# Thirteen input loads of a linear-attention kernel cut by partitions into 28 transfers

## The chip, the core and the metric

The kernel runs on one core of one Trainium2 chip. The core has five engines with queues of their own: TensorE (PE: matrix products, into PSUM), VectorE (DVE), ScalarE (ACT), GpSimd (POOL) and SyncE (SP), which here only issues transfers. Sixteen DMA engines move data between the chip's memory (HBM) and SBUF, the on-chip memory of 128 partitions. The metric is the device time of one execution in microseconds (us); less is better.

## What is computed

Two layers, one after the other: a decaying linear attention over 768 positions for 4 batches and 8 heads of 64, then a token mixer and a projection on its result.

```python
# attention: q, k, v are (4, 8, 768, 64)
for t in range(S):
    state = gamma[None, :, None, None] * state + np.einsum('bhd,bhe->bhde', k[:, :, t], v[:, :, t])
    y[:, :, t] = scale * np.einsum('bhd,bhde->bhe', q[:, :, t], state)
# x = y as (4, 768, 512); mixer:
W_tok = scale * np.einsum('bsd,btd->bst', x @ w_q, x @ w_k)
mixed = np.einsum('bst,btd->bsd', W_tok, x)
return np.maximum(mixed, 0.0) @ w_out
```

## The kernel before

The 768 positions of each batch are taken in three pairs of chunks of 128 positions, which makes twelve pairs, numbered 0 to 11; three pairs in a row belong to one batch. For each pair p the kernel needs three inputs, here called kp, qp and vp (k6 is the k input of pair 6). Each is one load of 512 KB into a staging buffer of 128 partitions: partition g holds positions 2g and 2g + 1 of the pair for all eight heads, so a partition gets eight pieces of 512 bytes. A partition of a load is called a row below.

A pair then goes through these steps. `ck`, `cq` and `cv` (L301, L329, L313) cast the loads to bf16, v with its decay factor; `ck` and `cv` come in two halves, and half c reads partitions 64c to 64c + 63 of the load (`rows(c)`). `trk` and `trq` transpose on PE and `ekT` evicts. `sc` and `eat` make the masked scores, `st` and `es` the running state, `ia` and `in` the output, `ex` takes it out of PSUM. `xt`, `exT`, `wqk`, `ew`, `zm`, `ez`, `mx` and `r` are the mixer, and `pj` and `eo` the projection with `w_out`. `stored` (L619) writes a pair's result, 512 KB, to HBM.

Nothing is scheduled automatically. `ORDER` (L16) is a list of all steps written out by hand; the letter behind a step names its engine (A for ACT, V for DVE, P for POOL), and each engine runs its own steps in the order of the list. SP's queue is written out in `LOADS` (L56): first all loads, with w (the mixer's two small weights) and o (`w_out`, in four transfers) between them, and at the end the stores s0 to s11. `more_loads` (L181) takes tokens off this list as long as the next one may go: a load of q, k or v needs a staging buffer, of which there are eighteen (`STAGES`), and a store needs its result evicted. The first k load is issued in halves, one from ACT and one from SP. On SP a transfer also waits until the transfer eight places before it has landed, since eight semaphores serve all of them in turn.

The helper that casts records its line as L135 (ACT) or L136 (POOL, DVE); `cv` is L318; loads are issued at L154, w at L162 and L163, o at L166, stores at L629.

Of the kernel before, what the change touches and what calls it, by code (L numbers as in the profile page):

```python
# [53 lines left out]


LOADS = """  # L56
q0 v0 k1 q1 v1 k2 q2 v2 w k3 q3 v3 k4 q4 v4 k5 q5 v5 o k6 q6 v6 k7 q7 v7 k8 q8 v8 k9 q9 v9 k10
q10 v10 k11 q11 v11 s0 s1 s2 s3 s5 s4 s6 s7 s8 s9 s10 s11/0 s11/1
""".split()

# [5 lines left out]
def kernel(  # L66
# [15 lines left out]
    nc = tc.nc  # L82
# [4 lines left out]
    C = 128  # L87
# [4 lines left out]
    HP = H // 2  # L92
# [51 lines left out]
    wk_stage = wstage_pool.tile([128, NDM, DH], FP32, name="wk_stage")  # L144
    wout_stage = wstage_pool.tile([128, NDM, DM], FP32, name="wout_stage")

    def load(name, p, half=None, eng=None):
        src = {"k": k, "q": q, "v": v}[name]
        b, cp = divmod(p, NP)
        st = pairs[p]  # L150
        if name + "_st" not in st:
            st[name + "_st"] = stage_pool.tile([128, 2, HP, 2, D], FP32, name=name + "_st", tag="st")
        xs = slice(0, 2) if half is None else slice(half, half + 1)
        dma = (eng or nc.sync).dma_start(  # L154
            out=st[name + "_st"][:, xs].rearrange("g x hp j d -> g (x hp) (j d)"),
            in_=src[b, xs.start * HP : xs.stop * HP, cp * 2 * C : (cp + 1) * 2 * C, :].rearrange(
                "h (g j) d -> g h (j d)", j=2
            ),
        )
    def load_token(token):  # L160
        if token == "w":
            nc.sync.dma_start(out=wq_stage, in_=moe_w_q.rearrange("(a p) h -> p a h", p=128))  # L162
            nc.sync.dma_start(out=wk_stage, in_=moe_w_k.rearrange("(a p) h -> p a h", p=128))  # L163
        elif token == "o":
            for a in range(NDM):
                nc.sync.dma_start(  # L166
                    out=wout_stage[:, a], in_=moe_w_out[128 * a : 128 * a + 128, :], max_dma_last_dim=512
                )
        else:
            load(token[0], int(token[1:]))  # L170

    load("k", 0, 0, nc.scalar)
    load("k", 0, 1, nc.sync)

    queue = list(LOADS)
    staged = ["k0"]
# [4 lines left out]
    def more_loads():  # L181
        while queue:
            token = queue[0]
            if token[0] == "s":
                if not stored(token[1:]):
                    return
                queue.pop(0)
                continue
            if token not in "wo":
                n = len(staged)  # L190
                if n >= STAGES and staged[n - STAGES] not in cast:
                    return
                staged.append(token)
            load_token(queue.pop(0))

    parts = {}
# [1 line left out]
    def release(token, n):  # L198
        parts[token] = parts.get(token, 0) + 1
        if parts[token] == n:  # L200
            cast.add(token)
            more_loads()

    more_loads()


# [7 lines left out]
    for h in range(H):  # L214
        x, hp = divmod(h, HP)
# [393 lines left out]
    def eo(e, b, p, j):  # L609
        st = pairs[p]  # L610
        if "o" not in st:
            st["o"] = ost_pool.tile([128, 2, DM], FP32, name="o_st")
        copy(e, st["o"][:, j], st["o_ps", j])
        evicted.add((p, j))
        more_loads()
# [3 lines left out]
    def stored(name):  # L619
        p, _, j = name.partition("/")  # L620
        p, js = int(p), [int(j)] if j else [0, 1]
        if not all((p, i) in evicted for i in js):
            return False
        b, cp = divmod(p, NP)
        dst = out[b, cp * 2 * C : (cp + 1) * 2 * C, :].rearrange("(g j) m -> g j m", j=2)
        src = pairs[p]["o"]
        if j:
            dst, src = dst[:, int(j)], src[:, int(j)]
        nc.sync.dma_start(out=dst, in_=src, max_dma_last_dim=512)  # L629
        return True  # L630
# [7 lines left out]
    for token in ORDER:  # L638
        token, _, b = token.partition("@")
        token, _, e = token.partition(":")  # L640
# [38 lines left out]
```

## Time and profile before

| | us |
|---|---|
| median of 3 runs | 98.48 (98.37 to 99.06) |
| the profiled execution | 98.37 |
| its span, first to last instruction | 96.6 |
| PE, DVE, ACT, POOL busy | 84.3, 75.1, 71.6, 59.5 |
| HBM read, written | 20.19 MB, 6.29 MB |
| a load, median from issue to landing | 6.3 (q), 6.5 (v), 6.4 (k) |

The profile is one execution on the chip. Its page gives, among other things, the busy tenths of each engine in 40 slices of 2.4 us, the busy share of the DMA engines and the rate that they moved (GB/s), the DMA queues, and the chain of work that ended last, followed back from the end. q1 is SP's queue, q10 ACT's, q8 and q14 carry instructions. In a timeline, a line gives the start, the duration, the engine, the line, the operation, the tiles, how many, and in brackets the idle time before it with what ended it. [...]

### The profile page before, as it was taken

To read this page: it belongs to the slowest core of one execution; us is meant where nothing else is said; L and a number is where in the kernel's file an instruction comes from. 1 tells how busy PE (TensorE), PEld (TensorE's weight loads), DVE (VectorE), ACT (ScalarE), POOL (GpSimd) and SP (SyncE) were. 2 spreads that over 40 slices of the span, in tenths; PEclk is the share of its full clock that TensorE was granted. 3 is DMA by queue.
4 is the path that set the end of the run, shared out by engine and by line. 5 is a ranking of instruction groups with operands and counts; after the bars stand their busy time and mean duration, and the time that the engine had idled before them with its cause. 6 is when DMAs were issued, how large, how long until landed. Compare 5 with 4: busy or idle time off the path is not lost.

```text
span 96.6 us, 3839 instructions
## 1 busy us (share of the span) xinstructions
PE 84.3 (87%) x1657; PEld 54.0 (56%) x1657; DVE 75.1 (78%) x108; ACT 71.6 (74%) x113; POOL 59.5 (62%) x74
## 2 busy tenths in 40 slices
PE   4999879897896789599999899999789999999920
PEld 1344355576765558256856546867776686534400
DVE  3035879999997999995798989989879997318640
ACT  4273999589797795597979999999999867454300
POOL 6610379494797997949999999999999500000000
PEclk9999999999999999999999999999999999999999
DMA  1999999989999999999999999999999980072995
GB/s 23 263 347 347 345 347 337 283 262 338 294 303 324 320 317 293 290 283 288 329 308 284 271 351 331 292 266 339 348 339 346 317 249 2 0 224 78 324 317 153
DMA packets 53137, 26.73 MB, mean 277 GB/s; under 512 B 1920, under 2 KB 53120, under 8 KB 53120
## 3 DMA queue, kind: packets, MB, share of 16 engines
q1 hardware_dynamic: 52592, 26.22, 92.3%
q10 hardware_dynamic: 528, 0.26, 0.9%
q8 instruction: 13, 0.21, 0.8%
q14 instruction: 4, 0.03, 0.1%
HBM read 20.19 MB, written 6.29 MB: 274 GB/s over the span
## 4 chain that ended last, share of the span: by engine, by line
SPq 22%; PE 22%; DMA 13%; POOL 12%; ACT 11%; DVE 10%; issue 6%; POOLq 0%; ACTq 0%; DVEq 0%
SPq L154 20%; DMA v_st<-in_v_dram 13%; PE banks L600 11%; POOL vs L318 8%; ACT ks L135 4%; POOL ks L136 4%; DVE at_sb L412 4%; DVE o_st L136 3%; ACT relu L593 2%; SPq L162 2%; PE banks L400 2%; PE banks L578 2%; PE banks L525 1%; ACT w_x L135 1%; PE banks L506 1%
## 5 line engine op out<-in xcount | busy, mean ns | idle before, releaser
L318 POOL TENSOR_TENSOR vs<-v_st,fv 64x512 bf16<-64x512 f32 x44 | 46.0, 1045 | 8.0 <-DMA v_st<-in_v_dram 3.6
L412 DVE TENSOR_TENSOR at_sb<-banks,cmask 128x1024 bf16<-128x1024 f32 x24 | 28.6, 1217 | 1.8 <-PE banks L400 1.3
L135 ACT CAST ks<-k_st 64x512 bf16<-64x512 f32 x38 | 23.4, 617 | 4.4 <-DMA k_st<-in_k_dram 3.8
L600 PE MATMUL banks<-wout_sb,relu 128*128 128x512 bf16 x96 | 23.3, 380 | 0.4 <-POOL wout_sb L136 0.4
L488 DVE TENSOR_TENSOR x_nat<-banks,fy 128x1024 bf16<-128x1024 f32 x12 | 14.6, 1220 | 1.6 <-PE banks L440 1.4
L600 PEld LDWEIGHTS <-relu 128*128 128x128 bf16 x96 | 8.2, 98 | 9.9 <-issue 1.4
L294 PE MATMUL banks<-warm 128*128 128x512 bf16 x41 | 12.6, 440 | 1.3 <-DVE warm L209 1.3
L593 ACT ACTIVATE relu<-banks 128x1024 bf16<-128x1024 f32 x9 | 9.3, 1028 | 2.2 <-PE banks L578 2.1
L135 ACT COPY o_st<-banks 128x512 f32<-128x512 f32 x15 | 8.7, 590 | 2.8 <-PE banks L600 2.8
L400 PE MATMUL banks<-qT,kT 64*128 64x128 bf16 x192 | 8.5, 216 | 1.3 <-ACT relu L593 0.8
L474 PE MATMUL banks<-vs,at_sb 128*128 128x64 bf16 x192 | 8.3, 194 | 0.4 <-DVE at_sb L412 0.4
L136 DVE COPY o_st<-banks 128x512 f32<-128x512 f32 x9 | 6.1, 686 | 2.9 <-PE banks L600 2.9
L135 ACT CAST qs<-q_st 128x1024 bf16<-128x1024 f32 (+1 forms) x8 | 7.9, 994 | 0.4 <-DMA q_st<-in_q_dram 0.3
L135 ACT COPY xT<-banks 128x1024 bf16<-128x1024 bf16 x7 | 7.2, 1022 | 1.4 <-PE banks L506 1.2
L474 PEld LDWEIGHTS <-at_sb 128*128 128x128 bf16 x192 | 6.8, 98 | 1.8 <-DVE at_sb L412 0.5
L136 DVE COPY kT<-banks 128x1024 bf16<-128x1024 bf16 x9 | 6.2, 687 | 2.1 <-PE banks L358 1.0
L136 POOL CAST qs<-q_st 128x1024 bf16<-128x1024 f32 (+1 forms) x4 | 3.7, 932 | 6.5 <-DMA q_st<-in_q_dram 6.4
L525 PE MATMUL banks<-xT,wqk_w 128*128 128x256 bf16 x48 | 7.2, 273 | 0.5 <-ACT xT L135 0.4
L400 PEld LDWEIGHTS <-kT 64*128 64x128 bf16 x192 | 6.4, 94 | 2.3 <-issue 1.8
L135 ACT CAST s_sb<-banks 128x256 bf16<-128x256 f32 x13 | 4.9, 378 | 3.2 <-PE banks L454 3.2
L294 PEld LDWEIGHTS <-warm 128*128 128x128 bf16 x41 | 3.9, 110 | 6.0 <-issue 2.7
L454 PE MATMUL banks<-vs,ks 128*64 128x64 bf16 x160 | 6.3, 200 | 0.5 <-ACT s_sb L135 0.5
(56 smaller groups left out, 112.8 us busy)
## 6 DMA issues: line engine op xcount, KB each, us to landing
q_st<-in_q_dram SPq DMA_DIRECT2D x12, 512.0 KB, 6.3
v_st<-in_v_dram SPq DMA_DIRECT2D x12, 512.0 KB, 6.5
k_st<-in_k_dram SPq DMA_DIRECT2D x11, 512.0 KB, 6.4
out_dram<-o_st SPq DMA_DIRECT2D x11, 512.0 KB, 6.1
wout_stage<-in_moe_w_out_dram SPq DMA_DIRECT2D x4, 256.0 KB, 5.6
out_dram<-o_st SPq DMA_DIRECT2D x2, 256.0 KB, 2.7
k_st<-in_k_dram ACTq DMA_DIRECT2D x1, 256.0 KB, 4.3
k_st<-in_k_dram SPq DMA_DIRECT2D x1, 256.0 KB, 4.0
```

What stands on the lines that cost most here:

```text
L135: return nc.scalar.copy(out=out, in_=in_)
L136: return ENGINES[e].tensor_copy(out=out, in_=in_)
L154: dma = (eng or nc.sync).dma_start(out=st[name + "_st"][:, xs].rearrange("g x hp j d -> g (x hp) (j d)"), in_=src[b, xs.start * HP : xs.st ...
L294: nc.tensor.matmul(out=bank32(b), lhsT=warm[:, 0:128], rhs=warm, start=True, stop=True)
L318: ENGINES[e].tensor_tensor(out=st["vs"][rows(j), c].rearrange("p hp x d -> p x hp d"), in0=st["v_st"][rows(c), :, :, j], in1=fv[rows(c), p ...
L400: nc.tensor.matmul(out=ps[:, x, hi, c, :], lhsT=st["kT"][rows(x), hp, c, :], rhs=st["qT"][rows(x), hp, c, :], start=(hi == 0 and c == 0), ...
L412: ENGINES[e].tensor_tensor(out=st["at", half].rearrange("p x hi c t -> p (x hi c) t"), in0=st["at_ps", half].rearrange("p (n t) -> p n t", ...
L474: nc.tensor.matmul(out=y[:, x, c, hp, :], lhsT=st["at", half][:, x, hi, c, :], rhs=st["vs"][:, c, hp, x, :], start=first(p, x), stop=False ...
L488: nc.vector.tensor_tensor(out=st["x"].rearrange("p x c i n -> p (x c i n)").rearrange("p (m d) -> p m d", d=D), in0=st["y_ps"].rearrange(" ...
L525: nc.tensor.matmul(out=ps[:, 128:384], lhsT=wqk_sb[:, a, 0:128], rhs=st["xT"][:, a].rearrange("p c t -> p (c t)"), start=(a == 0), stop=(a ...
L593: nc.scalar.activation(out=dst, in_=st["mx_ps"], func=ACT.Relu)
L600: nc.tensor.matmul(out=bank32(b), lhsT=st["relu"][:, a, j, :], rhs=wout_sb[:, a, :], start=(a == 0), stop=(a == NDM - 1),)
```

## The change

Each load may now be cut by partitions into several transfers. In `LOADS` a token may carry the sizes: `v3:120.8` is a transfer of partitions 0 to 119 and one of the last 8. Thirteen of the loads, v3 to q5 and v6 to v8, get sizes from six patterns: 120+8, 112+8+8, 104+24, 108+20, 110+18 and 100+28. The pieces of a load follow each other in SP's queue. The places of the loads and stores in the list, `ORDER`, the buffers and the arithmetic are the same.

```diff
 LOADS = """
-q0 v0 k1 q1 v1 k2 q2 v2 w k3 q3 v3 k4 q4 v4 k5 q5 v5 o k6 q6 v6 k7 q7 v7 k8 q8 v8 k9 q9 v9 k10
+q0 v0 k1 q1 v1 k2 q2 v2 w k3 q3 v3:120.8 k4:112.8.8 q4:104.24 v4:108.20 k5:110.18 q5:100.28 v5 o k6 q6 v6:120.8 k7:112.8.8 q7:104.24 v7:108.20 k8:110.18 q8:100.28 v8:120.8 k9 q9 v9 k10
 q10 v10 k11 q11 v11 s0 s1 s2 s3 s5 s4 s6 s7 s8 s9 s10 s11/0 s11/1
 """.split()
...
-    def load(name, p, half=None, eng=None):
+    def load(name, p, half=None, eng=None, cuts=(128,)):
...
-        dma = (eng or nc.sync).dma_start(
-            out=st[name + "_st"][:, xs].rearrange("g x hp j d -> g (x hp) (j d)"),
-            in_=src[b, xs.start * HP : xs.stop * HP, cp * 2 * C : (cp + 1) * 2 * C, :].rearrange(
-                "h (g j) d -> g h (j d)", j=2
-            ),
-        )
+        g = 0
+        for n in cuts:
+            (eng or nc.sync).dma_start(
+                out=st[name + "_st"][g : g + n, xs].rearrange("g x hp j d -> g (x hp) (j d)"),
+                in_=src[
+                    b,
+                    xs.start * HP : xs.stop * HP,
+                    cp * 2 * C + 2 * g : cp * 2 * C + 2 * (g + n),
+                    :,
+                ].rearrange("h (g j) d -> g h (j d)", j=2),
+            )
+            g += n
...
-            load(token[0], int(token[1:]))
+            token, _, cuts = token.partition(":")
+            load(token[0], int(token[1:]), cuts=[int(n) for n in (cuts or "128").split(".")])
...
-                staged.append(token)
+                staged.append(token.partition(":")[0])
```

## The prediction

> **What bounds the kernel now.** I read the page first (busy slices, queues, chain of waits), then busy time by stretches, the DMA row around single holes, SP's issues, and the stretches of POOL and ACT where a cast stands next to a landing.
>
> ```profile
> DMA  1999999989999999999999999999999980072995
> GB/s 23 263 347 347 345 347 337 283 262 338 294 303 324 320 317 293 290 283 288 329 308 284 271 351 331 292 266 339 348 339 346 317 249 2 0 224 78 324 317 153
> ...
> q8 instruction: 13, 0.21, 0.8%
> ...
> SPq 22%; PE 22%; DMA 13%; POOL 12%; ACT 11%; DVE 10%; issue 6%; POOLq 0%; ACTq 0%; DVEq 0%
> ```
>
> The sixteen DMA engines have work nearly all the time up to slice 32, and a third of the chain that ended last is SP's queue and a landing. The GB/s row shows that the stream is not at its best all that time: 345 to 347 early on, then again and again under 300. q8 are 13 fetches of 16 KB of instructions; 0.8% of 16 engines over 96.6 us is 12.4 us, so about 0.95 us each, on an engine that also carries loads.
>
> ```profile
> core 0: us, PE busy (x) PEld busy (x) DVE busy (x) ACT busy (x) POOL busy (x), PEclk, DMA share, GB/s
> 6.00:14.00 8.00, 6.95 (x99) 3.52 (x98) 4.70 (x7) 5.92 (x10) 2.70 (x3) 1.00 1.15 346
> 21.00:32.00 11.00, 9.33 (x243) 7.06 (x236) 10.29 (x13) 9.00 (x16) 8.32 (x9) 1.00 1.07 316
> ...
> 39.00:51.00 12.00, 11.11 (x229) 7.23 (x230) 10.29 (x13) 9.68 (x16) 10.17 (x12) 1.00 1.03 300
> 51.00:64.00 13.00, 12.60 (x304) 8.43 (x297) 12.13 (x15) 12.77 (x20) 12.20 (x13) 1.00 1.01 297
> 64.00:74.00 10.00, 8.97 (x204) 6.57 (x202) 8.81 (x12) 9.87 (x16) 9.41 (x10) 1.00 1.14 341
> ```
>
> Up to 51 us loads arrive at 300 to 316 GB/s with every compute engine almost full; from 51 to 74 us ACT is idle for only 0.23 + 0.13 = 0.36 us, so what makes ACT late at 51 us stays late; after that the chain of waits is PE without a break from 72.5 to 92.3 us. The clock is 1.00 throughout.
>
> The next answer is the DMA row from 18 to 22 us, 0.1 us a slice:
>
> ```profile
> DMA  9999999997658352114786899999999999999999
> GB/s 320 356 351 346 325 356 351 346 300 220 185 164 164 97 102 82 46 41 113 215 210 184 256 348 338 307 333 353 353 338 343 353 348 343 481 328 333 328 312 328
> ```
>
> Fetch number one ran at 16 to 18 us. The hole comes about 2 us later, when the other engines run dry: the shortfall against 346 from 18.8 to 20.2 us adds up to 0.8 us of stream. [...]
>
> ```profile
> 15.14 0.69 SPq L154 DMA_DIRECT2D k_st<-in_k_dram  x1
> 15.87 2.43 SPq L154 DMA_DIRECT2D q_st<-in_q_dram  x1
> 18.35 0.83 SPq L154 DMA_DIRECT2D v_st<-in_v_dram  x1
> ```
>
> [...] From 20.7 to 50.8 us the queue moved 9.29 MB, 309 GB/s in 30.1 us; at 346 it would be 26.9 us. So 3.2 us are lost there, with five fetches.
>
> ```profile
> 40.01 2.16 POOL L318 TENSOR_TENSOR vs<-v_st,fv 64x512 bf16<-64x512 f32 x2
> 43.47 2.15 POOL L318 TENSOR_TENSOR vs<-v_st,fv 64x512 bf16<-64x512 f32 x2 [1.30 <-DMA v_st<-in_v_dram]
> ```
>
> ```profile
> 50.88 1.25 ACT L135 CAST ks<-k_st 64x512 bf16<-64x512 f32 x2 [0.15 <-DMA k_st<-in_k_dram]
> ```
>
> POOL waited 1.30 us for v6 (issued at 36.73, 6.60 us to landing: 43.33) and has no further wait for a load up to 76 us; ACT waited 0.15 us for k8 (issued at 43.41, 7.4 us: 50.80). These two landings have no slack. Others have: q8 lands at 52.30 and POOL casts it at 52.75.
>
> **The change part by part.**
>
> *Same work elsewhere.* PE, DVE, ACT and POOL hold the same instructions in the same order; no step moves and the stores keep their place. Some casts wait for two or three transfers instead of one; the queue waits in the chain are 0.02 and 0.04 us, so this is nothing against a cast of 0.6 to 1.05 us.
>
> *Fifteen more issues on SP.* Thirteen loads become 28 transfers. An issue that nothing holds took 0.37 us (the late stores), so 15 x 0.37 = 5.6 us of SP's time. [...] Cost 0. [...]
>
> *A shorter window.* Eight semaphores serve the transfers in turn, so each issue waits until the one eight places before has landed. Before, eight places are eight loads, 8 x 1.49 = 11.9 us, against 6.3 us to landing: never binding. After, the tightest spot is the rest of k5, which waits for the first piece of k4 with under three loads between, 4.3 us; a load lands 4.9 us after its issue has ended (v4: 23.02 + 1.48 to 29.43). So SP is held for about 0.6 us at such a spot. [...]
>
> *Uneven pieces.* A load is 128 rows of eight 512-byte packets. At 346 GB/s it takes 1.49 us (SP's issues start 1.49 us apart from 5.3 to 9.7 us), 8 rows on each engine, 0.186 us a row. An engine has no speed in reserve: in the answer for 19.60 to 19.74 us, where one or two engines are at work (37 GB/s), packets still come about 24 ns apart, as with sixteen (512 bytes at 346/16 GB/s). So whoever gets more rows is later, and idle neighbours do not help. How a piece is shared out the trace does not show. Bound below: shared perfectly, 0 extra rows. Bound above: the large pieces rounded up to whole rows on sixteen engines, and the rests on only eight of them. Up to the first piece of k8 (that is all its first cast needs, rows 0 to 63) this is 79 + 25 = 104 rows on the busiest engine instead of 11 x 8 = 88: 16 x 0.186 = 3.0 us. I take the value between, all sixteen engines and whole rows: each of the six patterns costs its busiest engine 9 rows instead of 8 (8+1, 7+1+1, and 7+2 four times). Up to v6 that is seven split loads, +7 rows, +1.3 us; up to the first piece of k8 it is ten times +1 and then 7 for 8, +9 rows, +1.7 us; up to q8 +12 rows, 2.2 us, less 0.45 us of slack. I take it because unsplit loads run at the pace of all sixteen.
>
> *The holes.* Their cost before is 3.2 us up to k8. If the engine that fetches code is relieved, they shrink, at most by these 3.2 us; if it carries as much as any other, they stay. I keep them, since a piece of 100 to 120 rows on sixteen engines gives each engine about the same.
>
> [...]
>
> **Sum.** ACT is 1.7 us later at k8 and can swallow at most its 0.36 us of idle time by 74 us; POOL is 1.3 us later at v6 and 1.75 us at q8. The end is PE's, fed by both: +1.5 us. The profiled execution took 98.37 us (span 96.6 and 1.8 around it), 0.1 under the median of 98.48: 98.37 + 1.5 = 99.9 us.
>
> **The rivals.**
>
> *Faster: the holes close.* If the relieved engines include the one that fetches code, and pieces are shared well, up to 3.2 us of stream come back. For: a hole of 0.8 us behind a fetch is in the row above. Against: DVE is idle for only 0.71 us in 21 to 32 and 1.71 us in 39 to 51, and POOL can gain only what it waits, 1.30 us at v6 and 0.64 us for wout before. So at most about -1.7 us, 96.7 us. It decides from the point where the relief exceeds the extra rows by 1 us at v6 and k8.
>
> *No difference.* The pieces are shared evenly (0 rows, holes kept), or relief and extra rows cancel: 98.4 us. For it: most of the split loads land before their cast's turn comes, and the holes cost more (3.2 us) than nine rows do (1.7 us). Against it: the two would have to cancel at v6 and at k8 alike.
>
> *Much slower: few engines do the rests.* 3.0 us at k8 plus 0.6 us of held SP, less 0.36: +3.2 us, 101.6 us; more if several small pieces land late.
>
> **How the numbers follow.** Forecast 99.9 (99.4 to 101.0): 0.42. Much slower, 101.0 to 103.5: 0.16. No difference, 97.5 to 99.4: 0.24. Faster, 95.9 to 97.4: 0.18. Under 1% a measurement of this kernel cannot tell from no change, so faster 0.18, same 0.24, slower 0.58. The range from 96.8 to 102.4 leaves out about half of the faster case and half of the much slower one.
>
> **What would show it.** Right: between 21 and 32 us and between 39 and 51 us the stream is under 300 GB/s while DMA has slices under 9; POOL's wait for v6 grows from 1.30 to about 2.5 us, ACT's for k8 from 0.15 to 1 us or more; SP's issues of rests stay near 0.4 us. Wrong: v6 lands before 43.3 us, or the holes behind the fetches are gone, or ACT has idle time after 51 us that swallows a late k8.

## The result and the profile after

The changed kernel takes 106.52 us (median of 4 runs, 105.46 to 107.08), the kernel before took 98.43 us beside it (98.07 to 99.06): 1.078 times the time, 95% interval 1.066 to 1.090. Slower, as forecast, but by 8 us and not by 1.5; the time lies above the range. The profiled execution took 106.06 us, with a span of 104.3 us. A kernel's executions scatter, and those with a lower granted clock of TensorE are mostly the longer ones (the unchanged kernel once took 103.68 us at a mean clock of 0.956), so a ratio below counts only executions within 1.5% of the kernel's quickest, and `first` and `all104`, with one such execution each, have a median alone.

First the page of the changed kernel: the DMA row, the rate and the chain by engine, 2.6 us a slice.

```profile
DMA  1999999999987999999988999999999994053995
GB/s 25 306 347 347 347 351 315 255 245 230 170 221 209 254 304 335 331 250 220 233 203 203 203 242 293 300 339 345 341 349 339 339 316 135 0 156 100 274 318 164
...
SPq 34%; PE 24%; DMA 18%; POOL 10%; ACT 4%; issue 4%; DVE 1%; POOLq 0%; ACTq 0%; DVEq 0%
```

The rate falls to 170 to 255 GB/s where the two groups of cut loads pass (slices 8 to 14 and 18 to 24) and is at 347 to 351 before the first group and at 339 to 349 after the second. The DMA row says little of it: nearly all its digits are 9. SP's queue now has a third of the chain.

The same stretches as shown of before, with the same columns:

```profile
core 0: us, PE busy (x) PEld busy (x) DVE busy (x) ACT busy (x) POOL busy (x), PEclk, DMA share, GB/s
6.00:14.00 8.00, 6.95 (x122) 3.75 (x120) 5.19 (x6) 5.91 (x11) 3.03 (x4) 1.00 1.15 347
21.00:32.00 11.00, 7.53 (x183) 5.63 (x182) 8.82 (x11) 8.20 (x14) 5.64 (x6) 1.00 0.99 216
39.00:51.00 12.00, 9.47 (x218) 6.21 (x211) 9.20 (x11) 7.60 (x12) 7.33 (x7) 1.00 1.10 279
51.00:64.00 13.00, 9.63 (x192) 6.24 (x192) 8.85 (x12) 9.07 (x15) 9.84 (x12) 1.00 0.95 225
64.00:74.00 10.00, 9.46 (x226) 6.29 (x225) 9.00 (x13) 9.85 (x16) 9.39 (x10) 1.00 1.08 322
```

The last two columns are to be read together. The share is the time that all packets took, divided by the window, over 16 engines (it can be above 1: packets of one engine overlap, they start about 24 ns apart and take 27); so 16 x 512 bytes x share / rate is the time that one packet takes. From 6 to 14 us it is 8192 x 1.15 / 347 = 27.1 ns, as before (1.15 at 346). From 21 to 32 us before it was 8192 x 1.07 / 316 = 27.7 ns; now it is 8192 x 0.99 / 216 = 37.5 ns, and from 51 to 64 us 34.6 ns. The loss has two parts: the share is 0.99 instead of 1.15 (engines stand idle, 0.86), and a packet takes 37.5 ns instead of 27.1 (0.72); 0.86 x 0.72 = 0.62 = 216 / 347. This time per packet is the number that the rest of the study goes by.

What waits for it, in the stretches of POOL and then ACT:

```profile
43.78 2.16 POOL L327 TENSOR_TENSOR vs<-v_st,fv 64x512 bf16<-64x512 f32 x2
49.47 2.15 POOL L327 TENSOR_TENSOR vs<-v_st,fv 64x512 bf16<-64x512 f32 x2 [3.54 <-DMA v_st<-in_v_dram]
...
61.25 1.04 POOL L136 CAST qs<-q_st 128x1024 bf16<-128x1024 f32 x1 [2.56 <-DMA q_st<-in_q_dram]
```

```profile
52.76 1.04 ACT L135 CAST qs<-q_st 128x1024 bf16<-128x1024 f32 x1 [0.83 <-DMA q_st<-in_q_dram]
...
55.60 0.37 ACT L135 CAST s_sb<-banks 128x256 bf16<-128x256 f32 x1 [1.80 <-PE banks L463]
...
57.40 1.25 ACT L135 CAST ks<-k_st 64x512 bf16<-64x512 f32 x2 [0.66 <-DMA k_st<-in_k_dram]
```

v6 lands at 49.35 us instead of 43.33, the first piece of k8 at 57.32 instead of 50.80, q8 at 61.10 instead of 52.30. The chain of work that ended last runs through q8's landing (start and duration in us):

```profile
53.87 7.23 DMA q_st<-in_q_dram
61.17 0.08 issue
61.25 1.05 POOL qs L136
```

Before, the same cast started at 52.75 us:

```profile
52.75 1.04 POOL L136 CAST qs<-q_st 128x1024 bf16<-128x1024 f32 x1
```

So POOL is 8.5 us later there. It waits for nothing from there to its last cast, in either kernel, and the span ends 7.7 us later (104.3 instead of 96.6): all but 0.8 us of the delay goes to the end.

SP's issues in the second group; a line is a load's two pieces, the second figure the time that they held SP's queue (SPq):

```profile
47.60 3.17 SPq L156 DMA_DIRECT2D v_st<-in_v_dram  x2
50.87 2.48 SPq L156 DMA_DIRECT2D k_st<-in_k_dram  x2
53.45 2.60 SPq L156 DMA_DIRECT2D q_st<-in_q_dram  x2
56.14 2.46 SPq L156 DMA_DIRECT2D v_st<-in_v_dram  x2
```

A load holds the queue for 2.5 to 3.2 us instead of the 1.45 us of a whole one. That can be the fifteen further issues, or SP waiting for slower engines; the experiments had to say which.

One more view of the trace: the records of landings on the eight semaphores. A whole transfer leaves sixteen (before, each semaphore has 112 for seven transfers). In the change, a transfer with fewer than sixteen leaves one record more, 0.1 to 0.2 us after its issue ends: 1029 records in all are 1003 landings and one more for each of 26 transfers. The landings are 15 for 120 rows, 16 for 112 and 128, 13 for 104, 12 for 108, 11 for 110, 10 for 100, and 8, 12, 10, 9 and 14 for the rests of 8, 24, 20, 18 and 28. The packets of under 512 bytes on the page go with them: 2027 instead of 1920, 107 more, and by these counts thirteen loads have 315 landings instead of 208. Below, a landing is taken for one DMA engine that has done its part, and the rows of a transfer for evenly shared among its engines (each of these counts divides its row count); that is a reading of the counts. Which of the sixteen engines take part the records do not say.

### The profile page after: what moved, and what is told of

Same layout as the page of the kernel before. It is cut to its first block, busy times and chain, and to the rows that moved or that the text cites. A ratio compares the mean times of both kernels' runs of the same rounds, so it can differ in the third digit from the quotient of the medians.

```text
span 104.3 us, 3860 instructions
## 1 busy us (share of the span) xinstructions
PE 84.3 (81%) x1657; PEld 54.0 (52%) x1657; DVE 75.5 (72%) x108; ACT 71.7 (69%) x113; POOL 59.5 (57%) x74
## 2 busy tenths in 40 slices
DMA packets 53244, 26.73 MB, mean 256 GB/s; under 512 B 2027, under 2 KB 53227, under 8 KB 53227
## 4 chain that ended last, share of the span: by engine, by line
SPq 34%; PE 24%; DMA 18%; POOL 10%; ACT 4%; issue 4%; DVE 1%; POOLq 0%; ACTq 0%; DVEq 0%
SPq L156 28%; DMA q_st<-in_q_dram 14%; PE banks L609 11%; POOL vs L327 7%; DMA wout_stage<-in_moe_w_out_dram 4%; SPq L174 3%; PE banks L483 2%; ACT qs L135 2%; POOL wout_sb L136 2%; PE banks L534 2%; PE banks L587 2%; SPq L170 2%; PE banks L565 2%; PE banks L515 1%; PE banks L463 1%
## 5 line engine op out<-in xcount | busy, mean ns | idle before, releaser
L421 DVE TENSOR_TENSOR at_sb<-banks,cmask 128x1024 bf16<-128x1024 f32 x24 | 28.5, 1216 | 2.5 <-PE banks L409 2.1
L303 PE MATMUL banks<-warm 128*128 128x512 bf16 x41 | 12.0, 422 | 1.3 <-DVE warm L218 1.3
L463 PEld LDWEIGHTS <-ks 128*64 128x64 bf16 x160 | 4.8, 110 | 8.2 <-issue 7.5
L379 PE MATMUL banks<-identity,qs 64*128 64x64 bf16 x192 | 4.9, 191 | 3.0 <-POOL qs L136 1.2
```

The costliest lines, as they stand in the source:

```text
L303: nc.tensor.matmul(out=bank32(b), lhsT=warm[:, 0:128], rhs=warm, start=True, stop=True)
L421: ENGINES[e].tensor_tensor(out=st["at", half].rearrange("p x hi c t -> p (x hi c) t"), in0=st["at_ps", half].rearrange("p (n t) -> p n t", ...
L463: nc.tensor.matmul(out=state_ps[rows(x), hp, :], lhsT=st["ks"][:, c, hp, x, :], rhs=st["vs"][:, c, hp, x, :], start=(cp == 0 and c == 0 an ...
```

## The experiments

The theories after the result: *rows* (the engines that take part, and the rows on the busiest one, set the time), *issues* (fifteen more issues and the eight semaphores hold SP), *any other shape is slow*, and *sharing* (engines that are at work together slow each other down, and by how much depends on how many rows each gets; an assumption of the author's).

### Each shape by itself: shapes and shapes2

```python
for n in SHAPES:                      # shapes: 128 120 112 110 108 104 100 96 64
    for i in range(6):
        nc.sync.dma_start(out=bufs[i][0:n], in_=rows_of(src, (turn // 3) % 12, n))
    ...                               # the group is awaited, then the next shape
```
```diff
-SHAPES = (128, 120, 112, 110, 108, 104, 100, 96, 64)
+SHAPES = (128, 104, 117, 120, 105, 126, 110, 99, 64)
...
+    pool.tile([128, 224], FP32, name="pad")
```

> Loads alone, the attention and the mixer left out (the output is whatever the loads brought): nine groups of six transfers of the same shape, of 128, 120, 112, 110, 108, 104, 100, 96 and 64 rows, each group begun when the one before has landed; read by stretches. Rows theory (an engine's pace per packet is always 23 to 24 ns, and a transfer uses as many engines as its landings count: 16, 15, 16, 11, 12, 13, 10, 16, 16): rows on the busiest engine 8, 8, 7, 10, 9, 8, 10, 6, 4, so six transfers stream for 8.9, 8.9, 7.8, 11.2, 10.1, 8.9, 11.2, 6.7, 4.5 us, and the rate while streaming is 346 GB/s times the engines in use over 16 (324 for 120 rows, 216 for 100 rows). Packet theory (packets of a transfer that is not 128 rows take about a third longer, as 37 ns against 28 ns in the profile of the changed kernel): the groups other than 128 rows take a third more than that, 110 GB/s less at 112 and 96 rows than at 128.

Measured in `shapes`, as the mean duration of the group's packets, in ns: 128 rows 32.6, 120 45.7, 112 34.7, 110 32.6, 108 27.5, 104 45.7, 100 31.9, 96 39.4 (64 rows ran into the stores and cannot be separated). Neither the number of engines nor the size of a transfer orders these. The 108 rows stand out: they alone are at full pace, and they alone give an engine nine rows (108 rows, twelve landings). So `shapes2` asked for the same numbers of engines with nine rows each:

> Loads alone again (attention and mixer left out), six transfers of each shape: 128, 104, 117, 120, 105, 126, 110, 99 and 64 rows. [...] Rows theory (pace the same for all): 104 and 117 rows both at 280 GB/s, 120 and 105 both at 324. Any-other-shape theory (every transfer that is not 128 rows has slow packets): 117 and 126 as slow as 104 and 120.

The middles of its first eight groups, 128, 104, 117, 120, 105, 126, 110 and 99 rows:

```profile
core 0: us, DVE busy (x) POOL busy (x), PEclk, DMA share, GB/s
4.00:11.00 7.00, 0.00 (x0) 0.00 (x0) 1.00 1.15 347
15.00:26.00 11.00, 0.00 (x0) 0.00 (x0) 1.00 1.01 203
30.00:39.50 9.50, 0.00 (x0) 0.00 (x0) 1.00 0.93 282
43.00:55.00 12.00, 0.00 (x0) 0.00 (x0) 1.00 1.15 230
59.00:66.50 7.50, 0.00 (x0) 0.00 (x0) 1.00 1.13 290
71.00:80.00 9.00, 0.00 (x0) 0.00 (x0) 1.00 1.00 303
83.00:95.00 12.00, 0.00 (x0) 0.00 (x0) 1.00 0.82 210
100.00:109.00 9.00, 0.00 (x0) 0.00 (x0) 1.00 0.78 235
```

The second and third rows decide. A block here is the rows of a transfer that fall to one engine. On the same thirteen engines blocks of eight rows take 8192 x 1.01 / 203 = 40.8 ns a packet, blocks of nine 8192 x 0.93 / 282 = 27.0 ns: with eight rows an engine has lost about a third of its pace (27.0 / 40.8 = 0.66). Six transfers of 117 rows were through in 11.2 us, six of 104 rows in 13.2 us, so the larger transfer is the quicker one. 120 rows (blocks of eight) take 41.0 ns, 126 (blocks of nine) 27.0, and 105 (blocks of seven, if fifteen engines share them as for 120) 31.9; on eleven engines 110 rows (blocks of ten) take 32.0 and 99 (blocks of nine) 27.2. The engines of the three fast shapes can also be estimated from the table: sixteen have a share of 1.15 at that pace, so 0.93, 1.00 and 0.78 are 12.9, 13.9 and 10.9 engines. "Rows" alone and "any other shape is slow" fall. That 128 rows took 32.6 ns in one run and 27.1 in the other is not explained: the buffers lie elsewhere without the pad, and the two ran on different chips.

### On which side: source

If the eight rows of an engine follow each other, the blocks of the thirteen engines also lie 8 x 512 = 4096 bytes apart in HBM. This kernel keeps the partitions and moves the rows in HBM apart.

```diff
-SHAPES = (128, 104, 117, 120, 105, 126, 110, 99, 64)
+SHAPES = ((128, 2), (104, 2), (104, 3), (104, 5), (117, 2), (117, 3), (128, 3), (128, 5), (128, 2))
...
-        return src[b, :, cp * 256 : cp * 256 + 2 * n, :].rearrange("h (g j) d -> g h (j d)", j=2)
+        return src[b, :, 0 : n * step, :].rearrange("h (g t) d -> g h (t d)", t=step)[:, :, 0:128]
```

> Loads only, without the computation; the stores write what lies in the buffers, so the output is not the reference's. Nine groups of six transfers: 128, 104, 104, 104, 117, 117, 128, 128, 128 rows, whose rows lie 512, 512, 768, 1280, 512, 768, 768, 1280, 512 bytes apart in DRAM (the packets stay 512 bytes, and each row goes to the same partition as before). With blocks of eight rows, 512 bytes apart, thirteen engines read at distances of 4096 bytes from each other, with blocks of nine 4608 bytes: so the slow pace of 104 rows could come from the source side as well as from the partitions written. Theory 'partitions': 104 rows take 38 to 46 ns a packet, 165 to 205 GB/s, at all three distances, and 117 rows 27 to 28 ns, 280 GB/s, at both. Theory 'source': 104 rows become as fast as 117 rows (27 to 28 ns, 280 GB/s) at 768 and 1280 bytes, or 117 rows become slow at 768.

Its groups two to six: 104 rows at 512, 768 and 1280 bytes, 117 rows at 512 and 768.

```profile
core 0: us, DVE busy (x) POOL busy (x), PEclk, DMA share, GB/s
...
15.00:25.50 10.50, 0.00 (x0) 0.00 (x0) 1.00 1.00 208
30.00:40.50 10.50, 0.00 (x0) 0.00 (x0) 1.00 1.01 203
46.00:56.00 10.00, 0.00 (x0) 0.00 (x0) 1.00 1.00 202
61.00:69.50 8.50, 0.00 (x0) 0.00 (x0) 1.00 0.93 282
74.00:82.50 8.50, 0.00 (x0) 0.00 (x0) 1.00 0.93 281
```

39 to 41 ns for blocks of eight at every distance, 27 ns for blocks of nine at both. The distance in HBM does not matter at these three values, which leaves the side of the partitions; that follows by exclusion, no run moved the partitions alone.

### The same engines, other cuts: even112, half64, byhead

All three keep 28 transfers. `even112` and `half64` put eight rows on each of sixteen engines; `byhead` cuts by heads, so that every transfer has 128 partitions. Each of the three has 2160 packets of under 512 bytes, 240 more than before, which is sixteen landings for each of the fifteen further transfers.

```diff
 even112
-... v3:120.8 k4:112.8.8 q4:104.24 v4:108.20 k5:110.18 q5:100.28 ...
+... v3:112.16 k4:96.16.16 q4:112.16 v4:112.16 k5:112.16 q5:112.16 ...
 half64
+... v3:64.64 k4:64.32.32 q4:64.64 v4:64.64 k5:64.64 q5:64.64 ...
 byhead
+... v3:7.1 k4:6.1.1 q4:7.1 v4:7.1 k5:7.1 q5:7.1 ...
-                out=st[name + "_st"][g : g + n, xs].rearrange("g x hp j d -> g (x hp) (j d)"),
+                out=st[name + "_st"][:, xs].rearrange("g x hp j d -> g (x hp) (j d)")[:, g : g + n],
```

> The same thirteen loads cut into the same number of transfers (28), but 112+16, and 96+16+16 for k4 and k7: every piece is a multiple of 16 rows and loads all sixteen engines alike, 8 rows a load. Rows theory: back to the time before, 98 to 99 us. Issue theory (more transfers, SP held by the eight semaphores): still 104 to 107 us. Packet theory: packets of pieces other than 128 rows a third longer, thirteen loads of 1.49 us by a third, up to +6.5 us, 102 to 105 us.

> The thirteen loads cut 64+64 (64+32+32 for k4 and k7): the same number of transfers (28) and the same 8 rows on each of sixteen engines as without a cut. Rows theory: 98 to 99 us. Issue theory: as in the run with 112+16, 101 to 102 us. [...]

> The thirteen loads cut by heads instead of partitions: 128 rows x 7 heads and 128 rows x 1 head (6+1+1 for k4 and k7), 28 transfers as in the change, sixteen engines, 8 rows each. Issue theory (more issues and the eight semaphores cost time by themselves): 100 us or more. Rows and sharing theories: 98 to 99 us, as before.

Measured: `even112` 101.56 us (ratio 1.029, 1.020 to 1.039), `half64` 101.79 us (1.031, 1.024 to 1.038), `byhead` 99.13 us (1.004, 0.9995 to 1.008). The stretch from 21 to 32 us, first of `byhead`, then of `half64`, with the columns of the changed kernel's table:

```profile
21.00:32.00 11.00, 9.26 (x244) 7.11 (x240) 10.61 (x12) 9.71 (x17) 7.12 (x8) 1.00 0.99 289
```

```profile
21.00:32.00 11.00, 7.80 (x191) 5.85 (x189) 8.99 (x11) 8.38 (x14) 5.78 (x6) 0.99 1.19 245
```

`byhead` has as many issues and semaphores as the change, and its packets take 28.1 ns: "issues" is refuted, up to the 0.8% that the interval leaves. `half64` has no engine with more rows than before and none idle, its share is 1.19, and still the rate is 245 GB/s, because a packet takes 39.8 ns. So nearly all its loss is pace. That its time is the 101 to 102 us of "issues" is chance, since `byhead` has as many. `even112` fits none of its forecasts well: slower than "rows" had it (98 to 99 us) and a little quicker than slow packets for every other shape (102 to 105 us).

### One pattern for all: all120, all104, all117

```diff
 all120
+... v3:120.8 k4:120.8 q4:120.8 v4:120.8 k5:120.8 q5:120.8 ...
 all104
+... v3:104.24 k4:104.24 q4:104.24 v4:104.24 k5:104.24 q5:104.24 ...
 all117
+... v3:117.11 k4:117.11 q4:117.11 v4:117.11 k5:117.11 q5:117.11 ...
```

> [...] Rows theory: +1 row a load, 13 x 0.186 = 2.4 us at most, 99.5 to 101 us. Packet theory: +2.4 us and up to a third on 1.49 us thirteen times, 103 to 107 us.

> All thirteen loads are cut 104 + 24, and nothing else differs from the change. By the landing counts of the changed kernel 104 rows go to 13 engines in blocks of eight rows and 24 rows to 12 engines in blocks of two: ten rows on the busiest engines instead of eight. [...] Theory 'rows' (only the count of rows on the busiest engine matters): 2 rows x 0.186 = 0.37 us a load, 3.7 us at k8: 101 to 103 us, the same as for 117 + 11.

> All thirteen loads are cut 117 + 11: 13 engines with blocks of nine rows, and 11 engines with one row, so ten rows on the busiest engines, on the same number of engines as for 104 + 24. Theory 'sharing': no collision in the large piece, 1.7 us + 0.2 us instead of 1.5 us a load, 4 us at k8: 101 to 103.5 us, clearly below 104 + 24. Theory 'rows': the same number, and equal to 104 + 24. Theory 'any shape but 128 is slow': about 106 us, as for 104 + 24.

Measured: `all120` 104.12 us (1.056, 1.044 to 1.068), `all104` 105.9 us (103.26 to 106.72), `all117` 103.35 us (1.048, 1.039 to 1.057). `all120` lies where slow packets had it, `all117` where "sharing" had it, and `all104` above the 101 to 103 us of "rows". The stretch from 21 to 32 us of `all104`, then of `all117`:

```profile
21.00:32.00 11.00, 7.48 (x183) 5.78 (x182) 8.84 (x11) 7.80 (x13) 5.57 (x6) 0.98 0.97 199
```

```profile
21.00:32.00 11.00, 8.69 (x219) 6.67 (x218) 9.52 (x13) 8.60 (x14) 5.87 (x7) 1.00 0.83 241
```

Both put ten rows on the busiest engines (13 and 12 landings a load in `all104`, 13 and 11 in `all117`: 2037 and 2024 packets of under 512 bytes). 39.9 ns a packet with blocks of eight, 28.2 with blocks of nine, and v8 lands at 64.24 against 58.29 us. Their times overlap in part, the streams do not. That `all117` is 4.8% slower although its packets are at full pace is the other part of the loss: its share is 0.83, since three engines have nothing to do in a large piece and the busiest have two rows more.

### One group alone: first and second

```diff
 first
+... v3:120.8 k4:112.8.8 q4:104.24 v4:108.20 k5:110.18 q5:100.28 v5 o k6 q6 v6 k7 q7 v7 k8 q8 v8 ...
 second
+... v3 k4 q4 v4 k5 q5 v5 o k6 q6 v6:120.8 k7:112.8.8 q7:104.24 v7:108.20 k8:110.18 q8:100.28 v8:120.8 ...
```

> Only the first six loads cut (v3 to q5), with the patterns of the change. If the two groups of loads add up, about half of the 8 us: 101.5 to 103 us. If the first group is absorbed by the slack of v5 and o behind it and only the second one counts: 99 to 100 us. [...]

> Only the second group of loads (v6 to v8) is cut, with the patterns of the change; v3 to q5 are whole. If each group costs by itself (the delay that the first group leaves is not swallowed before the second), this takes about half of the change's 8 us, 101 to 103.5 us, and the two parts add up to the change. If the first group's delay is swallowed by idle time between the groups and only the second counts, this takes the whole, 105 to 107 us. If the second group's delay is hidden behind work that the first group has already made late, it takes under 100 us.

Measured: `first` 103.86 us (101.89 to 105.68), `second` 101.83 us (100.66 to 104.3; ratio 1.025, 1.016 to 1.034). Each group costs by itself, so neither is hidden behind the other. In the profiled runs the last of the packets up to v8 starts 3.9 us later than before in `first`, 5.6 us in `second` and 8.5 us in the change: in the stream the two parts add up to a little more than the whole. Whether the times add up as well is open: the medians are 5.4 and 3.4 us above the kernel before, against 8.1 us for the change, but each scatters by 3.6 us and more.

### An attempt to relieve the late engine: relief126

The one faster rival rested on the engine that also fetches code. In whole loads one landing often comes late (k8 before: fifteen by 49.79 us, the last at 50.80). 126 rows leave fourteen landings, with nine rows for each engine, at full pace (27.0 ns in `shapes2`). Eight loads were cut 126 + 2 in the hope that the engine that fetches would be one of the two without a part in the large piece. No trace stood behind that hope. One row more in eight loads is 8 x 0.186 = 1.5 us, against the 3.2 us of the holes.

```diff
-q0 v0 k1 q1 v1 k2 q2 v2 w k3 q3 v3:120.8 k4:112.8.8 q4:104.24 v4:108.20 k5:110.18 q5:100.28 v5 o k6 q6 v6:120.8 ...
+q0 v0 k1 q1 v1 k2 q2 v2 w k3:126.2 q3 v3 k4:126.2 q4 v4 k5:126.2 q5 v5:126.2 o k6 q6:126.2 v6 k7 q7 v7 k8 q8:126.2 v8 k9 q9:126.2 v9 k10
+q10:126.2 ...
```

> [...] If every shape but 128 is slow: 102 us or more.

Measured: 100.88 us (1.023, 1.017 to 1.029). Slower, but the late engine was not left out. The first fetch ran from 16.38 to 17.31 us, and of the fourteen landings of k3's large piece thirteen had come by 19.70 us and the last at 20.78; before, fifteen of k3's had come by 19.69 us and the last at 20.71. So the engine that fetches seems to be one of the fourteen, and late landings show as well in pieces on thirteen engines (v3 in `all117`: twelve by 23.99 us, the last at 25.16). The run shows what eight cuts of 126 + 2 cost; what a relief of that engine would bring stays untested.

### What a cut load costs with its rests: mixed

```diff
-SHAPES = (128, 104, 117, 120, 105, 126, 110, 99, 64)
+SHAPES = """
...
+126.2 126.2 126.2 126.2 126.2 126.2
+126.2 128 126.2 128 126.2 128
+104.24 104.24 104.24 104.24 104.24 104.24
...
+120.8 112.8.8 104.24 108.20 110.18 100.28
+128 128 128 128 128 128
+""".strip().splitlines()
...
+            for n in [int(c) for c in cuts.split(".")]:
+                nc.sync.dma_start(out=bufs[i][g : g + n], in_=rows_of(src, (turn // 3) % 12, g, n))
+                g += n
```

> Loads only, without the computation; the stores write what lies in the buffers, so the output is not the reference's. Nine groups of six loads, each load with its rests: whole; 120.8; 126.2; 126.2 and whole in turn; 104.24; 117.11; 112.8.8; the six patterns of the change one after the other; whole. Streaming time of a load in a group, whole 1.5 us. Theory 'sharing': 120.8 takes 2.2 to 2.4 us, 126.2 1.7 to 1.9, 104.24 2.5 to 2.7, 117.11 1.9, 112.8.8 2.0 to 2.2, the six patterns 2.2 to 2.5; 126.2 in turn with whole ones 1.6 to 1.75, unless blocks of nine collide with the neighbouring whole load's map, and then 1.9 or more. Theory 'rows': 9 rows x 0.186 = 1.7 us for 120.8 and 112.8.8, 10 rows = 1.9 us for 126.2, 104.24 and 117.11, 1.7 to 1.9 for the six patterns, and 1.7 for 126.2 in turn with whole ones.

From the first to the last packet of a group, a sixth of it, in us a load: whole 1.71 (1.65 in the last group), 120.8 2.51, 126.2 2.01, 126.2 and whole in turn 1.88, 104.24 2.59, 117.11 2.25, 112.8.8 2.16, the six patterns 2.54. Each figure has some 0.2 us of a group's start and run-out in it, so the differences from whole count: +0.80, +0.30, +0.17 (0.34 for each cut load), +0.88, +0.54, +0.45, and **+0.83 us a load for the change's patterns**. The middles of groups two, three, five and six (120.8, 126.2, 104.24, 117.11):

```profile
core 0: us, DVE busy (x) POOL busy (x), PEclk, DMA share, GB/s
...
15.50:28.00 12.50, 0.00 (x0) 0.00 (x0) 1.00 1.14 214
32.50:42.50 10.00, 0.00 (x0) 0.00 (x0) 1.00 0.97 292
...
59.50:72.50 13.00, 0.00 (x0) 0.00 (x0) 1.00 0.98 211
77.00:88.00 11.00, 0.00 (x0) 0.00 (x0) 1.00 0.93 267
```

43.6 and 38.0 ns with blocks of eight, 27.2 and 28.5 ns with blocks of nine, so the rests change nothing in this. Less those 0.2 us the figures are within 0.15 us of what "sharing" had expected, and "rows" is too low for 120.8 (2.3 against 1.7 us). The whole loads between cut ones cost nothing extra (0.34 against 0.30), and 0.30 us lies between one more row on the busiest engines (0.186 us) and two (0.37 us); whether the two rows of the rest fall to engines of the large piece is not shown. Six of the cut loads of `relief126` stand up to v8, and 6 x 0.30 = 1.8 us is about the delay of its stream there (1.7 us in the table below).

### All of them together

Delay is when the 29,184th packet of 512 bytes on SP's queue starts (that is as many as its loads up to v8 have), against the 52.52 us of before. Rows are the further rows on the busiest engines up to v8, at 0.186 us each, by the landing counts above, on the author's assumption that all pieces have their busiest engines in common, which no run here shows; the rest is the delay less that. The time of a packet is that of 21 to 32 us.

| kernel | delay, us | rows | rows, us | rest, us | ns a packet |
|---|---|---|---|---|---|
| byhead | 1.0 | 0 | 0 | 1.0 | 28.1 |
| even112 | 3.8 | 0 | 0 | 3.8 | 34.4 |
| half64 | 5.3 | 0 | 0 | 5.3 | 39.8 |
| relief126 | 1.7 | 12 | 2.2 | -0.5 | 30.5 |
| all117 | 4.3 | 26 | 4.8 | -0.5 | 28.2 |
| all120 | 6.2 | 13 | 2.4 | 3.8 | 42.2 |
| all104 | 8.6 | 26 | 4.8 | 3.8 | 39.9 |
| the change | 8.5 | 31 | 5.8 | 2.7 | 37.5 |

Where packets take 28 to 31 ns, the rows explain the delay within 1 us; where they take 34 to 42 ns, 2.7 to 5.3 us come on top. By this reckoning, an estimate, the change's delay is about two thirds rows on few engines and one third pace (the 1.0 us that `byhead` loses by its issues would count under the latter).

Why blocks of eight, ten, seven, six and four rows are slow (32 to 46 ns) and blocks of nine are not (27 to 29 ns), no run shows. That engines get in each other's way as they write was the author's assumption; it does not say how slow a block is, and it does not cover whole loads: they too give each of sixteen engines eight rows and run at 27 ns (32.6 in `shapes`). Shown is that on the same engines the number of rows for each decides the pace (40.8 and 27.0 ns on thirteen), and that the distance in HBM does not.

## Why the prediction was right in sign and wrong in size

- *What bounds the kernel* was right: the stream. Of 8.5 us of delay at POOL's cast of q8, 7.7 us became span. That the last load, v11, also lands 7.7 us later (76.96 instead of 69.26) is chance, since nothing waits for it.
- *Same work elsewhere, fifteen more issues, a shorter window, all at 0*: nearly right. That further issues are covered by waits of SP no run shows; in its place `byhead`, with as many issues, bounds the three together at 0.8% of the time. With late landings the window did bind once in the change: SP had issued v7's first piece by 48.00 us and the rest only at 49.37, when v6's first piece, eight transfers before, had landed (49.35); the DMA row has nearly all its digits at 9 there. The tell-tale was ill chosen: issues of rests were to stay near 0.4 us and many took 1.1 to 2.2 us, but in `byhead`, which loses little, they took up to 1.75 us too.
- *Uneven pieces, +1.3 us at v6, +1.7 us at the first piece of k8*: this step failed. Measured were +6.0 and +6.5 us. Two assumptions in it are refuted. "All sixteen engines and whole rows" gave +9 rows up to k8; by the landing counts the busiest engine had 112 instead of 88, +24 rows, 4.5 us, which is 2.8 us of the miss, if it is the same engine in every load (assumed, not shown). And the pace was taken as one number for all shapes, 0.186 us a row, from whole loads and from a window in which one or two engines were at work; in the cut loads a packet took 37.5 ns instead of 27.1, which is left for the other 2.0 us. The upper bound (+16 rows, 3.0 us) rounded on sixteen engines, so it was no bound, and neither bound looked at the pace. That whole loads run at the pace of all sixteen says nothing of a transfer of 104 rows, and the profile before has none: each of its 56 transfers leaves sixteen landings.
- *The holes, kept*: not separated. No run relieves the engine that fetches, so it is open whether any of the 3.2 us can be had that way. Nor does a trace show how a fetch (0.88 us from 16.34 us) leads to a hole about 2 us later.
- *The rivals.* "Faster" and "no difference" are out as outcomes. "Much slower" named the place rightly (few engines for a piece), for the rests alone and at 101.6 us; it was also the large pieces that went to few engines (ten to fifteen landings).
- *What would show it.* The stream is under 300 GB/s in both stretches (216 and 279), POOL waits 3.54 us for v6 (2.5 forecast). ACT's wait for k8 is only 0.66 us (1 us or more forecast), because ACT was late by then already: it had waited 0.83 us for q7 and 1.80 us for PE. And "DMA with slices under 9" hardly shows: busy engines do not mean engines at their pace.

## What to carry to other kernels

Cut a load along its free dimension rather than along partitions: 28 transfers of 128 partitions cost 0.4% here, 28 transfers that cut off 64 to 120 partitions and load the rest apart 3 to 8%. Where partitions must be cut, take two things from a trace of the transfer: how many landings it leaves (15 for 120 rows, 13 for 104 and 117 here), and how many rows that gives each engine; 126 or 117 rows (nine each) ran at 27 to 28 ns a packet, 120 or 104 (eight each) at 38 to 46. And read the DMA share together with GB/s: 16 x the packet's bytes x share / rate is the time of a packet, and it tells engines that wait from engines that are slowed down.

## What the runs showed of the hardware

- The pace of the DMA engines depends on the shape of the transfer: on thirteen engines a 512-byte packet takes 27.0 ns with nine rows for each (117) and 40.8 ns with eight (104).
- A larger transfer can be quicker than a smaller one: 117 rows 1.9 us each, 104 rows 2.2 us (11.2 and 13.2 us for six).
- The distance of the rows in HBM, 512, 768 or 1280 bytes, made no difference (208, 203, 202 GB/s).
- Fetches of instructions seem to hold up an engine that also carries loads: after one of 0.9 us a single landing of k3 came 1.0 us behind the others in the kernel before (fifteen by 19.69 us, the last at 20.71) and 1.1 us in `relief126`.
- TensorE's granted clock can fall in the middle of an execution, in the profiled one of `all117` to a half for 6.8 us (0.72 on average from 39 to 51 us); no run here shows why.
